# Expert 7 for the first 256 tokens, moved from the routing to the end of the program, and the last group's sums joined on VectorE

## The chip, the cores and the metric

One Trainium2 chip, one of its cores. The metric is the device time of one execution in microseconds (us); lower is better. All data are float32.

## The reference

Polysketch attention over 4 batches x 4 heads x 1088 tokens gives x, 4352 tokens x 128 features. A router then weighs all 8 experts for every token (Sinkhorn iterations), and every expert is computed for every token:

```python
logits = x @ w_gate                     # 4352 x 8
P = np.exp(logits - logits.max())
for _ in range(8):
    P /= P.sum(1, keepdims=True) + 1e-09
    P /= P.sum(0, keepdims=True) + 1e-09
    P *= N / E
for e in range(E):                      # w1[e]: 128 x 1024, w2[e]: 1024 x 128
    out += P[:, e:e + 1] * (np.maximum(x @ w1[e], 0.0) @ w2[e])
```

P is positive, so a token can be weighed before the first layer or after the second; the kernel does both, in different places.

## The kernel before

x is kept with features on partitions (`xT`, 128 x 4352). The expert work is cut in two.

**The unweighted items** (`groups`, `steps()`). They need no P, so they run on TensorE between the pieces of the attention and of the Sinkhorn routing; `fill(n)` and, after the routing, a loop take them step by step. Expert 0 is done here for all tokens. The first 256 tokens (`REST`) are done here for the experts 1 to 7 as well, one small item each of eight steps (order: 1, 2, 4, 3, 5, 6, 7). In a step `first` multiplies 128 of the 1024 hidden rows (line 787, ScalarE's Relu in line 789), and `second` multiplies the hidden rows of eight steps earlier (line 851). The last two items (`HELD = 2`, experts 6 and 7) keep their second products back: `held_product` (line 866) issues them among the weighted units. The sums land in `kept` (expert 0) and `kept_small` (experts 1 to 7); P weighs them much later (`rest_weigh`, on GpSimd), and `rest_out` turns them on VectorE and stores them, in the middle of the weighted part.

**The weighted units** (`weighted_events`). The other 4096 tokens go through the experts 1 to 7 in 8 groups of 512 tokens: 56 items, 112 units. Each unit uses a form of Strassen's seven products in both layers: `first_product` (line 1086), `taps` on ScalarE and VectorE (lines 1095 to 1107), `hsums` (lines 1113 to 1121), `second_products` (line 1136). All events have keys, and sorting the keys writes the program order of TensorE, VectorE and ScalarE; a period of 14 keys is one unit. Each engine runs its list strictly in that order, with semaphore waits where data or a PSUM bank is shared. GpSimd and SyncE also run in program order, but ahead of the others as far as their waits let them.

The combined weights that the seven products need ("forms") are made by `form_step`, four VectorE operations for each half of an expert (line 1048), and stored by `keep_formed`. Five halves (`AHEAD`) are made just before the weighted part, in the loop after the routing; six more (`IN_PLACE`) among the weighted units. `first_forms` (lines 988 to 992) makes the inputs of the first weighted item, from P as it comes back from DRAM (`pT`).

At the end of a group its sums lie in four PSUM banks (`ysums`) and have to be joined. For the groups but the last this is `group_end`, on ScalarE and VectorE while TensorE goes on. For the last group two copies and two additions bring them to SBUF (lines 1187, 1181), TensorE joins them with matrices of ones and zeros (`make_joins`, `join`, line 1237), VectorE turns the result (line 1213), and four transfers store it (line 757).

Names in the rows: `a` are the four banks of first products, `s` the four of second products, `w1f` and `w2f` the forms, `w2r` raw second weights, `hb` and `ht` hidden rows, `mid` a scratch tile.

Of the kernel before, what the change touches and what calls it, by code (L numbers as in the profile page):

```python
# [53 lines left out]
def kernel(  # L54
# [545 lines left out]
    def routing():  # L600
# [31 lines left out]
        for it in range(ITERS):  # L632
            rs = sk.tile([P, SA], F32, tag="rs", name="rs")
            nc.vector.reduce_sum(rs, pw, axis=AX.X)
            nc.vector.reciprocal(rs, rs)
            p1 = p1s[it % 2]
            nc.vector.scalar_tensor_tensor(p1[:, 0:SA], rs.unsqueeze(2).to_broadcast([P, SA, E]), UP,
                                           pw[:, :, 0:E], op0=Alu.mult, op1=Alu.mult)
            cs = sk.tile([P, E], F32, tag="cs", name="cs")
            nc.vector.reduce_sum(cs, p1.rearrange("p g e -> p e g"), axis=AX.X)  # L640
            yield 4.25
            pc = bank()[:, 0:E]
            for s in range(2):
# [236 lines left out]
    def steps():  # L880

        todo, sums_at, t = {}, {}, 0
        for k in range(len(blocks)):
            if k < len(blocks):
                j, q = blocks[k]
                g, e = items[j]
                n = groups[g][1]
                if q == 0:
                    prepare_w(j)
                if j == 0 and q == 2:  # L890
                    prepare_w(2)
                if j == 3 and q == 2:
                    small_load(2, wb[:, 3 * F:4 * F], wb[:, 4 * F:5 * F])
                if j == 7 and q == 0:
                    small_load(7, None, wb[:, 4 * F:5 * F])
# [41 lines left out]
    ENDING = {2: 42.6, 5: 43.6, 0: 46.6, 4: 47.6, 16: 50, 17: 51}  # L937
    X1, X2, Y1, Y2, T1, T3, T2, T4 = range(8)
    H0, H3, C12, H2_, D0, D1, D2 = range(7)
    D3 = C12  # L940
# [53 lines left out]
    def small_weights():  # L994

        spare = [pools[0].tile([P, 7, 2, NX], F32, tag="ht", name="ht").rearrange("p s a n -> p (s a n)") for _ in range(2)]
        xf0 = xfs[0].rearrange("p f n -> p (f n)")
        places = {3: (spare[0], 0, 1), 5: (spare[1], 0, 1), 4: (xf0, 0, 1)}
        for e, (t, i, k) in places.items():
            small_load(e, t[:, F * i:F * (i + 1)], t[:, F * k:F * (k + 1)])  # L1000
        small_load(6, spare[0][:, 2 * F:3 * F], wb[:, 5 * F:6 * F])
        small_load(7, spare[1][:, 2 * F:3 * F], None)

    def small_load(e, w1, w2):
        if w1 is not None:
# [158 lines left out]
    def rest_out(step):  # L1164
        yt = mid[:, 8 * NX:8 * NX + REST]
        if step:
            store(yt.rearrange("p (b d) -> p b d", d=32), 0, REST // 32, (nc.gpsimd,))
        else:
            nc.vector.transpose(out=yt, in_=kept[:, 0:REST])

    def group_end(g, step):

# [31 lines left out]
        elif step == 13:  # L1204
            add(y[upper, 0], z[upper, 2], z[upper, 1])
        elif step == 14:
            add(y[upper, 1], z[upper, 2], z[upper, 0])
        elif step == 15:
            y = y.rearrange("p s n -> p (s n)")
            add(y, y, kept[:, lo:lo + 2 * n])  # L1210
        elif step == 16:
            yt = turned_y[g] = mid[:, 4 * NX + 2 * NX * (g % 2):][:, 0:2 * n].rearrange("p (b d) -> p b d", d=32)
            nc.vector.transpose(out=yt.rearrange("p b d -> p (b d)"), in_=fbanks[0][:, 0:2 * n] if g == len(wgroups) - 1 else y.rearrange("p s n -> p (s n)"))
        elif step == 17:
            store(turned_y[g], lo // 32, (lo + 2 * n) // 32, (nc.gpsimd,) if g < len(wgroups) - 1 else (nc.sync, nc.scalar))

    turned_y, joins = {}, {}

    def make_joins():

        t = joins["t"] = mid[:, 4 * NX:6 * NX]
        tc.keep_in_program_order(nc.gpsimd.memset(t, 0.0))
        for half, lo, hi in ((lower, 0, 2), (lower, 3, 5), (upper, 3, 6), (upper, 7, 8)):
            tc.keep_in_program_order(nc.gpsimd.tensor_copy(
                t[half, H2 * lo:H2 * hi].rearrange("p (a d) -> p a d", d=H2),
                ident[half, half].unsqueeze(1).to_broadcast([H2, hi - lo, H2])))

    def join(g, step):

        lo, n, es = wgroups[g]  # L1230
        z = wb[:, 5 * F:5 * F + 4 * n].rearrange("p (s n) -> p s n", n=n)
        y = fbanks[0][:, 0:2 * n]

        def add(form, x, out, halves=(0, 1)):
            w = ident if form is None else joins["t"][:, H2 * form:H2 * form + P]
            for s in halves:
                nc.tensor.matmul(out[rows[s]], w[:, H2 * s:H2 * (s + 1)], x, start=x is kept_y, stop=True,  # L1237
                                 tile_position=(0, H2 * s), skip_group_check=True)

        kept_y = None  # L1240
        if step == 0:
            kept_y = kept[:, lo:lo + 2 * n]
            add(None, kept_y, y)
        elif step == 1:
            add(6, z[:, 2], y[:, 0:n], (1,))
            add(4, z[:, 2], y[:, n:])
            add(2, z[:, 3:4].to_broadcast([P, 2, n]), y.rearrange("p (a n) -> p a n", n=n), (1,))
        elif step == 2:
            add(0, z[:, 0], y[:, 0:n])
            add(3, z[:, 0], y[:, n:])  # L1250
            add(None, z[:, 1], y[:, 0:n])

    def weighted_events():
        out = []
# [23 lines left out]
        for k in range(len(units)):  # L1278
            b = PERIOD * k
            for r in range(2):  # L1280
                for m in AT:
                    if m in FIRST:
                        at(b + SHIFT * r + AT[m], first_product, k, r, m)
                    elif m in ("tm1", "tm5", "tu2", "rel", "c12", "c22"):
                        at(b + SHIFT * r + AT[m], taps, k, r, m)
                t, tasks = b + S_AT, list(range(7)) if k in firsts or k in lasts[:-1] else [6, 0, 4, 5, 1, 2, 3] if k == lasts[-1] else [0, 1, 6, 4, 5, 2, 3]
# [5 lines left out]
                at(b + (30.5 if m == "ts2" and k == len(units) - 2 else AT[m]), hsums, k, m)  # L1292
            if k in lasts:
                g = unit_of(k)[2]
                for n, key in (AFTER if k < lasts[-1] else ENDING).items():
                    at(b + key, group_end, g, n)
                if k == lasts[-1]:
                    at(b + 10, make_joins)
                    for n, key in enumerate((47.5, 48, 49)):
                        at(b + key, join, g, n)  # L1300
            if k in firsts:
                g = unit_of(k)[2]
                for step in range(wgroups[g][2][0]):
# [2 lines left out]
        for e in range(E):  # L1306
            at(420 + 28 * e, rest_weights, e)
            at(434 + 28 * e, rest_weigh, e)
        for step in range(2):
            at(660 + 14 * step, rest_out, step)  # L1310
        for n in range(2 * len(held)):
            at(HELD_AT + HELD_STEP * n, held_product, n)
        for n in range(HELD):
# [2 lines left out]
            at(end, held_sum, n)  # L1316
        return sorted(out, key=lambda x: x[:2])

    work = steps()
    owed, ran = [0.0], [0]  # L1320

# [30 lines left out]
    with tc.manual_schedule(engines={engines.DVE, engines.PE}):  # L1352
# [35 lines left out]
        forming = [lambda e=e, half=half, n=n: form_step(e - 1, half, n) for e, half in AHEAD for n in range(4)]  # L1388
        for n, (e, half) in enumerate(AHEAD):
            forming.insert(5 * n + 4, lambda e=e, half=half: keep_formed(e - 1, half))  # L1390
# [50 lines left out]
```

## Time and profile before

| | |
|---|---|
| Median of 3 runs | 904.93 us (902.96 to 906.27) |
| The profiled execution | 902.61 us, of which the span of the profile is 900.6 us |
| TensorE (PE) busy | 891.1 us, 99% of the span |
| VectorE (DVE), ScalarE (ACT), GpSimd (POOL) busy | 739.4, 526.2, 361.4 us |
| First weighted product | starts at 199.94 us |
| Last product, end of the joins, end of the span | 891.80, 895.84, 900.65 us |

A row of the timeline gives the start, the duration, the engine, the line of the kernel, the operation, the tile written and the tiles read, the shape, how many such instructions were merged into the row, and, in brackets, how long the engine had been idle before and whose end released it. One float32 product is two MATMUL entries. Their durations overlap, so a rate is read from the distance of starts.

### The profile page before, as it was taken

The page shows a single profiled execution, that of the slowest core. Times are in us where ns is not written, and L with a number is a line of the kernel's source. Part 1 is how long each engine was busy: PE and PEld are TensorE (multiplying, and loading weights), DVE is VectorE, ACT ScalarE, POOL GpSimd, SP SyncE. Part 2 cuts the span into 40 slices and gives each one's busy share as a digit, 9 for nine tenths or more (in the row PEclk, how much of TensorE's full clock was granted, in tenths as well). Part 3 has the DMA queues.
Part 4 walks back from the last instruction along what each step waited for, and adds up shares of the span by engine and source line. Part 5 has one row for each costly group of instructions (what it writes and reads, how often), then busy time and mean ns, then how long its engine had stood idle before and what let it go on. Part 6 is the DMA issues. An engine that isn't in the chain of part 4 may idle for free.

```text
span 900.6 us, 34646 instructions
## 1 busy us (share of the span) xinstructions
PE 891.1 (99%) x14664; PEld 718.5 (80%) x14664; DVE 739.4 (82%) x1160; ACT 526.2 (58%) x1276; POOL 361.4 (40%) x381
## 2 busy tenths in 40 slices
PE   8999999999999999999999999999999999999997
PEld 6786667688886998887878888778788887888885
DVE  7667678886889889799889988998888798889874
ACT  3353446465665765666666566666666666666562
POOL 3013310040444535366656454345443543544340
PEclk9999999999999999999999999999999999999999
DMA  9998492134677777677877767667776776777640
GB/s 260 295 284 271 151 330 75 42 148 135 172 211 246 240 222 218 210 217 209 241 232 218 222 206 217 201 214 222 218 221 188 219 218 206 234 212 218 188 127 13
DMA packets 150234, 183.97 MB, mean 204 GB/s; under 512 B 16352, under 2 KB 112368, under 8 KB 149696
## 3 DMA queue, kind: packets, MB, share of 16 engines
q1 hardware_dynamic: 143856, 164.17, 62.0%
q0 software_dynamic: 5024, 17.42, 5.6%
q8 instruction: 116, 1.90, 0.8%
q14 instruction: 38, 0.31, 0.1%
q10 hardware_dynamic: 1200, 0.16, 0.1%
HBM read 148.38 MB, written 18.65 MB: 185 GB/s over the span
## 4 chain that ended last, share of the span: by engine, by line
PE 96%; DVE 2%; DMA 1%; ACT 0%; SPq 0%; issue 0%; ACTq 0%; DVEq 0%
PE a L1086 37%; PE s L1136 37%; PE a L787 9%; PE s L851 8%; PE a L371 1%; PE s L866 1%; PE a L486 1%; DMA qx<-in_q_dram 1%; PE a L1237 0%; PE s L400 0%; PE a L450 0%; PE a L338 0%; DMA xd<-xt 0%; DMA xT<-xd 0%; PE s L416 0%
## 5 line engine op out<-in xcount | busy, mean ns | idle before, releaser
L1086 PE MATMUL a<-wb,w1f 64*64 64x256 f32 x4144 | 430.7, 377 | 0.1
L1086 PEld LDWEIGHTS a<-wb,w1f 64*64 64x64 f32 x4144 | 277.6, 133 | 34.0 <-issue 2.0
L1086 PE MATMUL a<-xf,w1f 64*64 64x256 f32 x2128 | 229.9, 377 | 0.1
L1100 ACT COPY a<-a 128x256 f32<-128x256 f32 x224 | 80.0, 357 | 214.2 <-PE a L1086 214.2
L1136 PE MATMUL s<-ht,w2r 64*64 64x256 f32 x1344 | 192.1, 377 | 0.0
L1136 PE MATMUL s<-hb,w2r 64*64 64x256 f32 x1344 | 190.7, 376 | 0.0
L201 POOL TENSOR_TENSOR wb<-wb 128x256 f32<-128x256 f32 (+1 forms) x115 | 127.9, 1113 | 121.6 <-DMA wb<-wb 106.8
L1136 PE MATMUL s<-ht,w2f 64*64 64x256 f32 x1216 | 159.6, 376 | 0.3 <-DVE w2f L1048 0.3
L1086 PEld LDWEIGHTS a<-xf,w1f 64*64 64x64 f32 x2128 | 142.5, 133 | 19.0 <-issue 1.1
L1136 PE MATMUL s<-hb,w2f 64*64 64x256 f32 x1216 | 157.5, 376 | 0.0
L1136 PEld LDWEIGHTS s<-ht,w2r 64*64 64x64 f32 x1344 | 113.9, 133 | 20.7 <-DVE ht L1121 0.4
L1136 PEld LDWEIGHTS s<-hb,w2r 64*64 64x64 f32 x1344 | 114.1, 133 | 18.6
L789 ACT ACTIVATE hb<-a 128x256 f32<-128x256 f32 (+3 forms) x152 | 66.2, 442 | 75.3 <-PE a L787 71.8
L1136 PEld LDWEIGHTS s<-ht,w2f 64*64 64x64 f32 x1216 | 100.1, 133 | 8.4 <-DVE w2f L1048 0.7
L1136 PEld LDWEIGHTS s<-hb,w2f 64*64 64x64 f32 x1216 | 99.7, 133 | 7.3
L787 PE MATMUL a<-xT,wb 128*64 128x416 f32 (+3 forms) x448 | 103.4, 459 | 0.0
L851 PE MATMUL s<-hb,wb 128*64 128x416 f32 (+3 forms) x408 | 99.8, 453 | 0.0
L201 POOL TENSOR_TENSOR xf<-xf 128x256 f32<-128x256 f32 (+1 forms) x62 | 69.0, 1116 | 70.4 <-DMA xf<-xf 50.2
L201 POOL TENSOR_TENSOR wb<-wb,xT 128x512 f32<-128x512 f32 x37 | 52.1, 1410 | 92.7 <-DMA wb<-pT 62.9
L1107 DVE TENSOR_TENSOR ht<-a,mid 128x256 f32<-128x256 f32 x112 | 47.2, 422 | 49.0 <-ACT a L1095 39.5
L1095 ACT COPY a<-a 128x256 f32<-128x256 f32 x224 | 80.0, 357 | 9.6 <-PE a L1086 1.0
L1098 ACT COPY mid<-a 128x256 f32<-128x256 f32 x224 | 84.7, 378 | 0.0
(203 smaller groups left out, 1648.5 us busy)
## 6 DMA issues: line engine op xcount, KB each, us to landing
w1f<-packed SPq DMA_DIRECT2D x204, 224.0 KB, 5.1
w2r<-in_moe_w_dram SPq DMA_DIRECT2D x56, 512.0 KB, 7.0
w2f<-packed SPq DMA_DIRECT2D x68, 256.0 KB, 5.0
wb<-pT SPq DMA_DIRECT2D x45, 256.0 KB, 4.5
wb<-wb SPq DMA_DIRECT2D x74, 128.0 KB, 4.0
hb<-packed SPq DMA_DIRECT2D x32, 256.0 KB, 6.4
xf<-pT SPq DMA_DIRECT2D x19, 256.0 KB, 4.5
xf<-xf SPq DMA_DIRECT2D x36, 128.0 KB, 4.3
```

Source lines behind the costliest of these rows:

```text
L201: tc.keep_in_program_order(nc.gpsimd.tensor_tensor(*args, op=op))
L371: nc.tensor.matmul(pv[64 * s:64 * (s + 1), i], kp[0:n, H * t + h].rearrange("p i j -> p (i j)"), vx[0:n, slots[h], t, :], start=(t == 0 an ...
L486: nc.tensor.matmul(pn[64 * s:64 * (s + 1), t, 2 * i:2 * i + 2].rearrange("p h d -> p (h d)"), ph[:, i, s, 64 * t:64 * (t + 1)], kvs[b % 2] ...
L787: nc.tensor.matmul(ph[sl], loaded_w[items[j][1]][0][:, P * f + H2 * s:P * f + H2 * (s + 1)], xT[:, lo:hi], start=True, stop=True, tile_pos ...
L789: nc.scalar.activation(out=out, in_=ph, func=Act.Relu)
L851: nc.tensor.matmul(sums[g][i][H2 * s:H2 * (s + 1)], w, x, start=c == 1, stop=c == per, tile_position=(0, H2 * s))
L1086: nc.tensor.matmul(half_of(r, b, c, n)[rows[s]], w1s[i][rows[r], 1 + form, u, H2 * s:H2 * (s + 1)], xf(i, x)[rows[r]], start=m == opens, s ...
L1095: nc.scalar.copy(b, a)
L1098: nc.scalar.copy(m5s[k, r], c)
L1100: nc.scalar.copy(d, a)
L1107: nc.vector.tensor_tensor(h[:, H3, r], d, m5s[k, r], op=Alu.add)
L1136: nc.tensor.matmul(place[rows[s]], w[form][rows[r], pair, u], h[rows[r], x, pair], start=task in (0, 4) and k in firsts, stop=True, tile_p ...
```

## The change

Expert 7 is taken out of the unweighted items, which leaves twelve of them, and the held items are now those of the experts 5 and 6. Its 256 tokens are now weighed before the first layer (`rest_weigh` writes them to a free part of `kept_small`). Its weights are loaded near the end into a part of `kept` that is free by then (`closing_load`). Four of its eight first products (`closing_first`) stand among the second products of the last unit but one, four behind the last second product of all. Its second products (`closing_second`) take the hidden rows as the stationary side, so that the result has tokens on partitions; a product with the identity brings the sums of the other seven experts, `kept`, into the same bank. This is done for two blocks of 128 tokens, and `closing_out` copies each block and stores it in four transfers. `rest_out` in the middle goes.

The last group's sums are joined by `last_end`: six ScalarE copies and thirteen VectorE additions, then the same turning and four transfers as before (now two by SyncE and two by GpSimd). `make_joins` and `join` go.

The forms of `AHEAD` start earlier: one entry of the list in each Sinkhorn iteration from the third on, the rest from seven steps earlier than before; `first_forms` comes six steps earlier. In the units 10 and 12 the order of the second products is changed, so that task 6 (which uses the form `S3_`) comes after the tasks 4 and 5.

```diff
             nc.vector.reduce_sum(cs, p1.rearrange("p g e -> p e g"), axis=AX.X)
+            if it > 1:
+                forming.pop(0)()
             yield 4.25
...
-              (2752, 416, [0]), (0, REST, [4]), (3584, 384, [0]), *((0, REST, [e]) for e in (3, 5, 6, 7))]
+              (2752, 416, [0]), (0, REST, [4]), (3584, 384, [0]), *((0, REST, [e]) for e in (3, 5, 6))]
...
     def rest_weigh(e):
+        if e == E - 1:
+            pool(kept_small[:, e - 1], xT[:, 0:REST], rest_room[0], op=Alu.mult)
+            return
...
+    CLOSING_AT = (24, 27, 30, 33, 48, 48.2, 48.4, 48.6)
+    closing_w = (kept[:, 2 * NX:2 * NX + F], kept[:, 2 * NX + F:2 * NX + 2 * F].rearrange("p (f d) -> p f d", d=DM))
...
+    def closing_h(c):
+        return hts[len(units) - 4][:, REST * c:REST * (c + 1)]
+
+    def closing_first(c):
+        ph = fbanks[c % 3][:, 0:REST]
+        for s in range(2):
+            nc.tensor.matmul(ph[rows[s]], closing_w[0][:, P * c + H2 * s:P * c + H2 * (s + 1)], kept_small[:, E - 2],
+                             start=True, stop=True, tile_position=(0, H2 * s), skip_group_check=True)
+        nc.scalar.activation(out=closing_h(c), in_=ph, func=Act.Relu)
+
+    def closing_second(b, c):
+        for s in range(2):
+            x = P * b + H2 * s
+            nc.tensor.matmul(fbanks[3][rows[s], P * b:P * (b + 1)],
+                             kept[:, x:x + H2] if c < 0 else closing_h(c)[:, x:x + H2],
+                             ident if c < 0 else closing_w[1][:, c], start=c < 0 and not b, stop=True,
+                             tile_position=(0, H2 * s), skip_group_check=True)
+
+    def closing_out(b):
+        y = mid[:, 8 * NX + P * b:8 * NX + P * (b + 1)]
+        nc.scalar.copy(y, fbanks[3][:, P * b:P * (b + 1)])
+        for a in range(4):
+            (nc.sync, nc.scalar)[a % 2].dma_start(out=..., in_=y[32 * a:32 * (a + 1)])
+
+    LAST_AT = (42.1, 42.6, 42.7, 42.8, 43, 43.1, 43.2, 43.3, 43.4, 44.1, 44.6, 44.7, 44.8, 44.9, 45, 45.1, 45.2, 47.1, 47.6, 48.1, 48.2)
+
+    def last_end(g, step):
...
+        (lambda: nc.scalar.copy(z[:, 2:4], s[1]),
+         lambda: add(z[:, 2:4], z[:, 2:4], s[3]),
+         lambda: nc.scalar.copy(x[upper, 0], z[lower, 3]),
+         lambda: nc.scalar.copy(x[lower, 0], z[upper, 2]),
+         lambda: add(y[upper, 1], z[upper, 3], z[upper, 2]),
+         lambda: add(y[lower, 1], z[lower, 2], k[lower, 1]),
+         lambda: add(y[:, 1], y[:, 1], x[:, 0]),
+         lambda: add(y[upper, 0], y[upper, 1], k[upper, 0]),
+         lambda: add(y[upper, 1], y[upper, 1], k[upper, 1]),
+         lambda: nc.scalar.copy(z[:, 0], s[0][:, 0]),
+         lambda: add(z[:, 0], z[:, 0], s[2][:, 0]),
+         lambda: nc.scalar.copy(x[upper, 1], z[lower, 0]),
+         lambda: nc.scalar.copy(x[lower, 1], z[upper, 0]),
+         lambda: add(y[:, 1], y[:, 1], z[:, 0]),
+         lambda: add(y[lower, 0], z[lower, 0], k[lower, 0]),
+         lambda: add(y[upper, 0], y[upper, 0], x[upper, 1]),
+         lambda: add(y[:, 1], y[:, 1], x[:, 1]),
+         lambda: add(y[:, 0], y[:, 0], s[0][:, 1]),
+         lambda: add(y[:, 0], y[:, 0], s[2][:, 1]),
+         lambda: group_end(g, 16),
+         lambda: group_end(g, 17))[step]()
...
-    def make_joins():
-    def join(g, step):
...
+ ... [0, 1, 4, 5, 6, 2, 3] if k in (10, 12) else [0, 1, 6, 4, 5, 2, 3]
...
+                for half in range(2):
+                    at(b - 8 + 8 * half, closing_load, half)
+                for n, key in enumerate(CLOSING_AT):
+                    at(b + key, closing_first, n)
+                for n in range(2):
+                    for c in range(-1, FO):
+                        at(b + 49 + n, closing_second, n, c)
+                    at(b + 49 + n, closing_out, n)
...
-        for step in range(2):
-            at(660 + 14 * step, rest_out, step)
...
-        among = {t0 + 10: [first_forms],
+        among = {t0 + 4: [first_forms],
...
-            if ran[0] > t0 + 3 and forming:
+            if ran[0] > t0 - 4 and forming:
```

More of the change, by code (lines that the diff above doesn't have):

```diff
@@ L894, in steps @@
                 if j == 7 and q == 0:
-                    small_load(7, None, wb[:, 4 * F:5 * F])
+                    small_load(5, None, wb[:, 4 * F:5 * F])
                 if q == 1 and j + 1 < len(items) and not direct_of(j + 1):
@@ L936 @@
              16: 170, 17: 184}
-    ENDING = {2: 42.6, 5: 43.6, 0: 46.6, 4: 47.6, 16: 50, 17: 51}
     X1, X2, Y1, Y2, T1, T3, T2, T4 = range(8)
@@ L997, in small_weights @@
         xf0 = xfs[0].rearrange("p f n -> p (f n)")
[L998 to L1002, printed above, removed]
+        small_load(3, spare[0][:, 0:F], spare[0][:, F:2 * F])
+        small_load(5, spare[1][:, 0:F], None)
+        small_load(4, xf0[:, 0:F], xf0[:, F:2 * F])
+        small_load(6, spare[1][:, F:2 * F], wb[:, 5 * F:6 * F])
     def small_load(e, w1, w2):
@@ L1162, in rest_weigh, with closing_load @@
             pool(kept[:, 0:REST], kept[:, 0:REST], y, op=Alu.add)
[L1164 to L1167, printed above, removed]
-        else:
-            nc.vector.transpose(out=yt, in_=kept[:, 0:REST])
+    CLOSING_AT = (24, 27, 30, 33, 48, 48.2, 48.4, 48.6)
+    closing_w = (kept[:, 2 * NX:2 * NX + F], kept[:, 2 * NX + F:2 * NX + 2 * F].rearrange("p (f d) -> p f d", d=DM))
+    def closing_load(half):
+        w1, w2 = closing_w
+        if half:
+            load_w2(E - 1, w2)
+        else:
+            tc.keep_in_program_order(nc.sync.dma_start(out=w1, in_=moe_w1[E - 1]))
@@ new lines, in closing_out @@
+    def closing_out(b):
+        y = mid[:, 8 * NX + P * b:8 * NX + P * (b + 1)]
+        nc.scalar.copy(y, fbanks[3][:, P * b:P * (b + 1)])
+        for a in range(4):
+            (nc.sync, nc.scalar)[a % 2].dma_start(out=AP(tensor=out.tensor, offset=out[4 * b + a, 0].offset, ap=[[SA * DM, 32], [1, DM]]),
+                                                  in_=y[32 * a:32 * (a + 1)])
+    LAST_AT = (42.1, 42.6, 42.7, 42.8, 43, 43.1, 43.2, 43.3, 43.4, 44.1, 44.6, 44.7, 44.8, 44.9, 45, 45.1, 45.2, 47.1, 47.6, 48.1, 48.2)
@@ new lines, in last_end, with add @@
+    def last_end(g, step):
+        lo, n, es = wgroups[g]
+        if ("w", g) not in parts:
+            parts["w", g] = room("w", 2 * n)
+        z = wb[:, 5 * F:5 * F + 4 * n].rearrange("p (s n) -> p s n", n=n)
+        y = wb[:, 4 * F + F // 2:5 * F][:, 0:2 * n].rearrange("p (s n) -> p s n", n=n)
+        x = parts["w", g].rearrange("p (s n) -> p s n", n=n)
+        k = kept[:, lo:lo + 2 * n].rearrange("p (s n) -> p s n", n=n)
+        s = [ysums[g][b].rearrange("p (s n) -> p s n", n=n) for b in range(4)]
+        def add(out, a, b):
+            nc.vector.tensor_tensor(out, a, b, op=Alu.add)
+        (lambda: nc.scalar.copy(z[:, 2:4], s[1]),
[19 more added lines that the diff above has]
+         lambda: group_end(g, 17))[step]()
@@ L1212, in group_end @@
             yt = turned_y[g] = mid[:, 4 * NX + 2 * NX * (g % 2):][:, 0:2 * n].rearrange("p (b d) -> p b d", d=32)
-            nc.vector.transpose(out=yt.rearrange("p b d -> p (b d)"), in_=fbanks[0][:, 0:2 * n] if g == len(wgroups) - 1 else y.rearrange("p s n -> p (s n)"))
+            nc.vector.transpose(out=yt.rearrange("p b d -> p (b d)"), in_=y.rearrange("p s n -> p (s n)"))
         elif step == 17:
-            store(turned_y[g], lo // 32, (lo + 2 * n) // 32, (nc.gpsimd,) if g < len(wgroups) - 1 else (nc.sync, nc.scalar))
-    turned_y, joins = {}, {}
-    def make_joins():
[L1221 to L1226, printed above, removed]
-    def join(g, step):
[L1230 to L1251, printed above, removed]
+            store(turned_y[g], lo // 32, (lo + 2 * n) // 32, (nc.gpsimd,) if g < len(wgroups) - 1 else (nc.sync, nc.gpsimd))
+    turned_y = {}
     def weighted_events():
@@ L1285, in weighted_events @@
                         at(b + SHIFT * r + AT[m], taps, k, r, m)
-                t, tasks = b + S_AT, list(range(7)) if k in firsts or k in lasts[:-1] else [6, 0, 4, 5, 1, 2, 3] if k == lasts[-1] else [0, 1, 6, 4, 5, 2, 3]
+                t, tasks = b + S_AT, list(range(7)) if k in firsts or k in lasts[:-1] else [6, 0, 4, 5, 1, 2, 3] if k == lasts[-1] else [0, 1, 4, 5, 6, 2, 3] if k in (10, 12) else [0, 1, 6, 4, 5, 2, 3]
                 while tasks:
@@ L1294, in weighted_events @@
                 g = unit_of(k)[2]
[L1295 to L1300, printed above, removed]
+                if k < lasts[-1]:
+                    for n, key in AFTER.items():
+                        at(b + key, group_end, g, n)
+                    continue
+                for n, key in enumerate(LAST_AT):
+                    at(b + key, last_end, g, n)
+                for half in range(2):
[6 more added lines that the diff above has]
+                    at(b + 49 + n, closing_out, n)
             if k in firsts:
@@ L1317, in weighted_events @@
         return sorted(out, key=lambda x: x[:2])
+    forming = []
+    for e, i in AHEAD:
+        forming.extend(lambda e=e, i=i, n=n: form_step(e - 1, i, n) for n in range(4))
+        forming.append(lambda e=e, i=i: keep_formed(e - 1, i))
     work = steps()
@@ L1387 @@
         turn_first()
-        forming = [lambda e=e, half=half, n=n: form_step(e - 1, half, n) for e, half in AHEAD for n in range(4)]
-        for n, (e, half) in enumerate(AHEAD):
-            forming.insert(5 * n + 4, lambda e=e, half=half: keep_formed(e - 1, half))
-        among = {t0 + 10: [first_forms],
+        among = {t0 + 4: [first_forms],
                  t0 + 12: [lambda do=do: do(1) for do in (weights, weighted, turn, xsums)]}
```

## The prediction

> **What bounds the kernel now.** I read the page first: busy times, and the chain that ended last.
>
> ```profile
> PE 891.1 (99%) x14664; PEld 718.5 (80%) x14664; DVE 739.4 (82%) x1160; ACT 526.2 (58%) x1276; POOL 361.4 (40%) x381
> PE 96%; DVE 2%; DMA 1%; ACT 0%; SPq 0%; issue 0%; ACTq 0%; DVEq 0%
> ```
>
> TensorE (PE) carries the chain from end to end. So work that leaves PE is worth its full time, wherever it stood, as long as no other engine becomes late by it. Second, PE's waits; in the whole weighted part there are two:
>
> ```profile
> PE s L1136 <- DVE hb L1048: 1.1, 1, 1.1
> PE s L1136 <- DVE w2f L1048: 0.3, 1, 0.3
> ```
>
> Both are second products that wait for a form made by VectorE (DVE). Third, PE's timeline where the weighted part begins:
>
> ```profile
> 194.12 0.65 PE L787 MATMUL a<-xT,ht 128*64 128x256 f32 x4
> 194.55 0.65 PE L851 MATMUL s<-hb,ht 128*64 128x256 f32 x4
> 194.99 0.65 PE L787 MATMUL a<-xT,ht 128*64 128x256 f32 x4
> 195.42 0.65 PE L851 MATMUL s<-hb,ht 128*64 128x256 f32 x4
> 195.85 3.67 PE L787 MATMUL a<-xT,ht 128*64 128x256 f32 x32
> 199.45 0.66 PE L1407 MATMUL a<-zeros 64*64 64x256 f32 x8
> 199.94 0.38 PE L1086 MATMUL a<-xf,w1f 64*64 64x256 f32 x2
> ```
>
> By the distance of starts a step's first product (four entries) takes 0.43 us and its second product 0.43; nothing waits. Fourth, the other engines at the end (timeline):
>
> ```profile
> 890.19 0.59 ACT L1187 COPY wb<-s 128x512 f32<-128x512 f32 x1 [3.78 <-PE s L1136]
> 890.80 0.69 DVE L1181 TENSOR_TENSOR wb<-wb,s 128x512 f32<-128x512 f32 x1 [1.69 <-ACT wb L1187]
> 895.87 0.72 DVE L1213 STREAM_TRANSPOSE mid<-a 128x512 f32<-128x512 f32 x1 [3.08 <-PE a L1237]
> 896.61 0.88 SPq L757 DMA_DIRECT2D out_dram<-mid  x2
> 896.61 0.96 ACTq L757 DMA_DIRECT2D out_dram<-mid  x2
> ```
>
> The last products end at 891.80 and the joins at 895.84 (chain), turning ends at 896.59, the span at 900.65. By the table of stages the data of the last store move from 897.4 to 899.0, so 0.8 us pass before them and 1.6 behind them.
>
> **The change, part by part.** The profiled execution took 902.61, 2.0 over its span and 0.26% under the median of 904.93; I work in its times and carry the difference over to the median.
>
> *Front.* Item 7 leaves: eight steps of 0.43 + 0.43, so 6.9 us, and the first weighted product moves from 199.94 to about 193.0. Held products stay the same in number. What covers this: DVE must be through its own list when the first tap comes, 4.45 us after the first weighted product (the add of line 1107 started at 204.39), so at 197.5 now. From the last turning in the routing, which ended at 171.97, its list is six subtractions of line 802 (2.10 + 2.15), `first_forms` (4.3 with GpSimd beside it), six sums of group 8 (6 x 0.56, and 2.9 more, since one took 3.50 beside GpSimd) and 15 forms (0.34 to 0.42 each, 5.7): 20.6 us, so 192.5, or 198.7 if all 6.2 us of waits of before (0.86 + 3.34 + 1.96) came back. Since five forms more can fill these waits, I take no cost; the bounds are 0 and 1.2. Unit 0 itself needs only `first_forms`, whose P had landed by about 179; they should end near 183. GpSimd now stores two halves of forms ahead of the last sums for item 1, which should be ready by about 194 (two sums of 1.3 and 1.1 us each side of a 4 us transfer) and are needed at 205.
>
> *Forms in the routing.* Five DVE operations of 0.42 us, each behind the column sums of an iteration and ahead of three subtractions. PE's small product needs those sums, which are finished first: no wait. The reciprocal behind them can come 0.4 later; PE's next column product stood about 2 us behind its sums, so the five are hidden; unhidden they cost 2.1. They move the last turning, and P's way through DRAM, by 0.4; `first_forms` had about 10 us to spare.
>
> *Tasks 4 and 5 ahead of 6 in units 10 and 12.* The form that came too late is `S3_`, the last to be made there. Task 6 now comes four keys later, 1.7 us, against waits of 1.1 and 0.3: minus 1.4 (0 if another wait takes their place).
>
> *Middle.* One turning, four stores on GpSimd's queue and one GpSimd product go. None was on the chain: 0. Held copies, weights of expert 7 (two loads of 512 KB, queued behind the last w2f issued at 863.5, 7.0 us to landing, needed after 885): 0, with 14 us of cover.
>
> *End.* Times here are those of before, from which the 8.3 us above are taken off last. Unit 110's second products start at 884.74 and take 3.0. Among them now stand four closing first products, 4 x 0.43 = 1.7, and I add 0.4 for the changes between whole-height and half-height products (no row prices that; 0 to 0.8). Unit 111's thus start at 889.85 instead of 887.7, and the copy of the first pair of sums, 2.45 later, at 892.3. Call this T; before it was 890.19, and the last product ended at T + 1.6.
>
> Now comes what I hold to be the price of the change. In the order of the changed program, task 2 of row half 0 waits for the ScalarE (ACT) copy of the other half of the same bank, and task 2 of row half 1 for the DVE addition that reads its bank. Both stand deep in `last_end`. ACT: copy 0.59; DVE addition to T + 1.30; two copies (0.36, 0.27 apart) to T + 1.98; then the copy in question to T + 2.25. DVE: additions at T + 1.33, 1.67, 2.12 (waits for ACT's copy), 2.57, 3.02 (each needs the one before), and the one in question T + 3.36 to 3.78. So PE stops at about T + 0.7, does tasks 2 and 3 of one half from 2.3 to 3.15, stops again to 3.8, and ends the last product at T + 4.7 instead of 1.6: 3.1 us of waits.
>
> Behind it: four closing first products 1.7 (T + 6.4; ACT keeps up, the last Relu ends at 7.0); block 0, identity and eight products of 128 columns: 0.215 each, half the 0.43 of 256 columns, 1.95 (T + 8.35); ACT copy of 128 x 128, 0.25 by the slope between 0.36 for 256 and 0.59 for 512, with 0.2 ahead of it for the drain (T + 8.8); block 1 waits for that copy, since it uses the same bank, then 1.95 (T + 10.8); copy to T + 11.25; two issues on each queue, first 0.8 to the data, then 0.4 for a second issue and little data (256 pieces against 2112), then 1.6 to the end: T + 14.1 = 906.4. Against 900.65 that is plus 5.75. In it, the joins' 4.04 us on PE and the turning are gone. `last_end` itself ends at about T + 6.8 on DVE, its store near T + 10.5: hidden under the closing products, with 3 us of cover.
>
> Sum: -6.9 - 1.4 + 5.75 = -2.55, so 900.1 in profiled terms and 902.4 as median. The gain of the front is for the most part paid back at the end: PE's work of item 7 is not less there (3.44 + 3.87), only the joins are saved, and more than half of that goes into waits.
>
> **Rivals.** *The waits at the end do not bind* (the copy and the addition come earlier than I chain them, or part of the waits overlaps). Then the 3.1 us and block 1's 0.45 go: -6.1, 898.8. For it: PE has practically no wait in the profile of before, and nothing shows a stop at the end. Against: the waits are written in the program, and the durations come from rows.
>
> *The clock falls* (slower than before). After the joins PE has nothing to do, and the table of stages shows the granted clock (after PEclk's place, before the DMA share):
>
> ```profile
> 898.20:898.60 0.40, 0.00 (x0) 0.00 (x0) 0.00 (x0) 0.00 (x0) 0.00 (x0) 1.00 1.20 192
> 898.60:899.00 0.40, 0.00 (x0) 0.00 (x0) 0.00 (x0) 0.00 (x0) 0.00 (x0) 0.66 1.09 167
> 899.00:899.20 0.20, 0.00 (x0) 0.00 (x0) 0.00 (x0) 0.00 (x0) 0.00 (x0) 0.50 0.06 8
> ```
>
> It halves near 898.7, 2.9 us after PE stopped. If the stops of 1.6 and 0.65 us with little work between them are long enough for that, the 6.4 us of matmuls behind (0.85 + 1.7 + 3.9) take twice as long: +6.4, 908.8. It decides from a stop of about 2.9 us; I expect 1.6. The Trainium skill (TensorE: Matmul & The Clock Gate, Part 1) says that a free-running window of about 3.4 us without work halves the clock; the trace agrees with the half, and with the time as far as a free-running window allows, and by that rule two stops this short would not do it.
>
> *DVE is late at the start of the weighted part* (forms, or GpSimd beside DVE): PE waits at the first taps and the front gives 3 to 5 us instead of 6.9: 904.3 to 906.3. For it: additions in that stretch took 3.50 and 1.38 us where 0.55 and 0.42 are usual. Against: the count above leaves 5 us.
>
> *The reordering brings nothing* (the form is late all the same): +1.4, 903.8, inside the forecast.
>
> **How the numbers follow.** My forecast 0.64, waits that do not bind 0.18, late DVE 0.10, clock 0.06, else 0.02. About 0.5%, 4.5 us, is what a measurement of this kernel can tell from no change. Only the second case passes it on the fast side, and an end of the forecast's own spread (0 to 0.8, 0 to 1.2, chains read 1 us wrong); the clock case hardly reaches it on the slow side. Faster 0.20, same 0.73, slower 0.07. The range goes from the second case's lower side to the late DVE's upper side, 898.3 to 906.8.
>
> **What would show it.** First weighted product near 193; no wait of line 1136 for line 1048; in the last 15 us, PE waits of about 1.5 and 0.7 us at line 1136 for ACT and DVE, a wait of about 0.5 for the copy of line 1197, and 2.8 us from that line's last copy to the end. A first weighted product later than 194, a last stretch without those waits, or a clock below 1.00 ahead of the last store would each prove the step wrong that names it.

## The result, and the profile after

The changed kernel is slower by 0.5%: 910.67 us median of 7 runs (907.80 to 911.18) against 904.93 (902.96 to 908.21), a ratio of 1.0053, 95% interval 1.0032 to 1.0074. The forecast was 902.4, range 898.3 to 906.8, so it is missed on the slow side, by 8.3 us. The profiled execution took 907.80, its span 905.81: 5.2 over the one of before.

From the page, the busy line and the chain that ended last:

```profile
PE 896.1 (99%) x14680; PEld 720.3 (80%) x14680; DVE 744.0 (82%) x1170; ACT 527.7 (58%) x1281; POOL 362.3 (40%) x373
PE 95%; DVE 3%; issue 1%; ACT 1%; DMA 1%; SPq 0%; POOL 0%; ACTq 0%; DVEq 0%; POOLq 0%
```

TensorE still carries the chain, and it is busy 5.0 us longer than before, with 16 MATMUL entries (8 products) more. Busy time that grows by more than the work does points to the clock. PE's waits from 195 us to the end (line, releaser, sum, times, longest):

```profile
PE s L1136 <- ACT wb L1227: 2.1, 1, 2.1
PE s L1136 <- DVE wb L1216: 0.5, 1, 0.5
PE a L1190 <- ACT mid L1197: 0.4, 1, 0.4
PE a L1086 <- DVE ht L1107: 0.3, 1, 0.3
```

The two waits for line 1048 are gone, and three waits stand at the end, those that the prediction named. PE's timeline, the first weighted product and the end:

```profile
193.93 0.38 PE L1086 MATMUL a<-xf,w1f 64*64 64x256 f32 x2
890.18 1.56 PE L1136 MATMUL s<-hb,w2r 64*64 64x256 f32 x8 [2.07 <-ACT wb L1227]
892.22 1.97 PE L1136 MATMUL s<-hb,w2r 64*64 64x256 f32 x8 [0.47 <-DVE wb L1216]
894.12 3.58 PE L1183 MATMUL a<-kept,kept 128*64 128x256 f32 x16
900.03 0.44 PE L1190 MATMUL a<-ident,kept 128*64 128x128 f32 x4 [0.37 <-ACT mid L1197]
```

Read the durations: eight matmuls of 64 rows take 1.56 and 1.97 us, and four closing first products (16 entries) 3.58, where 0.43 each would make 1.7. ScalarE's rows for the copy of the first pair of sums (the prediction's T) and the last copy:

```profile
887.71 0.59 ACT L1218 COPY wb<-s 128x512 f32<-128x512 f32 x1 [1.49 <-PE s L1136]
902.26 0.27 ACT L1197 COPY mid<-a 128x128 f32<-128x128 f32 x1 [2.29 <-PE a L1190]
```

The table of stages (stretch, its length, then the busy time of PE, PEld, DVE, ACT and POOL, then the granted clock) says why. Its stretches are cut at the edges of the clock's record:

```profile
887.22:890.64 3.42, 1.35 (x24) 0.67 (x16) 1.80 (x4) 1.66 (x4) 0.00 (x0) 1.00 0.00 0
890.64:894.05 3.41, 2.94 (x14) 0.98 (x10) 3.21 (x9) 0.81 (x2) 0.00 (x0) 0.50 0.01 2
894.05:897.46 3.41, 3.41 (x18) 1.95 (x18) 1.27 (x3) 1.15 (x3) 1.29 (x2) 0.50 0.27 54
897.46:900.88 3.42, 3.05 (x54) 2.74 (x52) 0.00 (x0) 0.65 (x2) 0.00 (x0) 1.00 0.15 29
```

The clock is halved from 890.64 to 897.46, over almost all of the work that stands between the stop and the closing second products.

**Where the time went.** Spans of one kernel wander by some us, so I cut each profiled execution at three marks of PE: the first small product of the routing's iterations (line 644 before, 646 after), the first weighted product, and the start of the last weighted first product. Every run below is in the table.

| kernel | start to routing | to first weighted | weighted | end | span |
|---|---|---|---|---|---|
| before | 122.67 | 77.27 | 685.45 | 15.27 | 900.65 |
| after | 122.84 | 71.09 | 685.22 | 26.65 | 905.81 |
| e1_late | 124.23 | 71.06 | 684.91 | 21.30 | 901.51 |
| e2_busy | 123.82 | 71.06 | 685.87 | 24.15 | 904.90 |
| e3_no_routing_forms | 123.45 | 70.36 | 684.85 | 26.95 | 905.60 |
| e4_behind | 122.14 | 71.05 | 686.82 | 25.02 | 905.04 |
| e5_before_order | 122.90 | 77.28 | 686.21 | 15.27 | 901.66 |
| e6_both | 122.51 | 71.07 | 687.65 | 19.35 | 900.59 |
| e7_both_old_order | 123.52 | 71.07 | 686.40 | 19.37 | 900.36 |
| e8_busy_two | 124.46 | 71.07 | 687.47 | 25.82 | 908.82 |
| e9_both_no_forms | 122.27 | 70.36 | 687.11 | 19.42 | 899.17 |
| e10_copy_first | 123.29 | 70.37 | 684.78 | 17.96 | 896.39 |

The first and third columns scatter by 2 to 3 us among kernels that are equal there. The second repeats to 0.04 us among the kernels with one front, and the fourth to 0.3 where nothing at the end was changed. So the second and fourth are what can be explained: after against before, they are -6.18 and +11.38. (The expectations below give some ends from spans read to 0.1 us, which differ from the table by up to 0.06.)

### The profile page after: what moved, and what is told of

It is laid out like the page before. It is cut to its first block, busy times and chain, and to the rows that moved or that the text cites. A ratio compares the mean times of both kernels' runs of the same rounds, so it can differ in the third digit from the quotient of the medians.

```text
span 905.8 us, 34686 instructions
## 1 busy us (share of the span) xinstructions
PE 896.1 (99%) x14680; PEld 720.3 (80%) x14680; DVE 744.0 (82%) x1170; ACT 527.7 (58%) x1281; POOL 362.3 (40%) x373
## 4 chain that ended last, share of the span: by engine, by line
PE 95%; DVE 3%; issue 1%; ACT 1%; DMA 1%; SPq 0%; POOL 0%; ACTq 0%; DVEq 0%; POOLq 0%
PE a L1086 37%; PE s L1136 36%; PE a L789 8%; PE s L853 7%; PE a L371 1%; PE s L868 1%; PE a L486 1%; PE a L119 1%; PE a L1183 1%; PE a L1190 0%; PE a L338 0%; DVE hb L1115 0%; PE s L400 0%; PE a L450 0%; DVE hb L1121 0%
## 5 line engine op out<-in xcount | busy, mean ns | idle before, releaser
L1086 PEld LDWEIGHTS a<-wb,w1f 64*64 64x64 f32 x4144 | 271.4, 133 | 36.2 <-issue 3.2
L201 POOL TENSOR_TENSOR wb<-wb 128x256 f32<-128x256 f32 (+1 forms) x115 | 131.0, 1141 | 118.7 <-DMA wb<-wb 91.8
L1136 PEld LDWEIGHTS s<-ht,w2r 64*64 64x64 f32 x1344 | 113.6, 133 | 18.9
L791 ACT ACTIVATE hb<-a 128x256 f32<-128x256 f32 (+3 forms) x144 | 63.2, 445 | 72.9 <-PE a L789 69.9
L201 POOL TENSOR_TENSOR xf<-xf 128x256 f32<-128x256 f32 (+1 forms) x62 | 72.2, 1167 | 68.3 <-DMA xf<-xf 43.8
```

What stands on the lines that cost most here:

```text
L201: tc.keep_in_program_order(nc.gpsimd.tensor_tensor(*args, op=op))
L791: nc.scalar.activation(out=out, in_=ph, func=Act.Relu)
L1086: nc.tensor.matmul(half_of(r, b, c, n)[rows[s]], w1s[i][rows[r], 1 + form, u, H2 * s:H2 * (s + 1)], xf(i, x)[rows[r]], start=m == opens, s ...
L1136: nc.tensor.matmul(place[rows[s]], w[form][rows[r], pair, u], h[rows[r], x, pair], start=task in (0, 4) and k in firsts, stop=True, tile_p ...
```

## Experiments

A task, below, is one of the seven second products of a unit; TensorE does each for two row halves, and a half-height product uses only one of them. T is, as in the prediction, the start of the copy of the first pair of sums.

The theory after the result: the two bank waits stop TensorE, and this stop, though shorter than the 2.9 us that the prediction took as the point of decision, halves the clock. Rivals: the clock falls for another cause, or the end is longer only for the work that was moved there.

**e1_late: the waits taken away.** The copies and additions of `last_end` that the last tasks waited for come behind them in program order.

```diff
-LAST_AT = (..., 43.4, 44.1, 44.6, 44.7, 44.8, 44.9, 45, 45.1, 45.2, 47.1, 47.6, 48.1, 48.2)
+LAST_AT = (..., 43.4, 48.7, 48.71, 48.72, 48.73, 48.74, 48.75, 48.76, 48.77, 48.78, 48.79, 49.5, 49.5)
```

> Ten of the steps of last_end, from the copy after the first pair of copies on to the store, stand behind the four closing first products in the listed order, so that tasks 2 and 3 of unit 111 no longer wait for ScalarE or VectorE. Theory 1 (the two bank waits of 2.07 and 0.47 us stop TensorE, and the stop halves its clock for 6.83 us, 3.4 us of work): both waits go, the clock stays 1.00 up to the last product, and the profiled span falls by 2.5 + 3.4 = 5.9 us to about 900; less by up to 1 if last_end's store is then the last thing to land. Rival A (the halved clock has nothing to do with the wait and comes whatever is done at the end): only 2.5 go, 903.3. Rival B (the end is longer only for the work moved there): less than 1 us goes, 905.

Measured: 904.66 us, ratio to before 1.0006 (0.9995 to 1.0017). Both waits are gone, the clock stays at 1.00 to the last product, and the end shrinks by 5.35 us (the span by 4.3, since the first column happens to be 1.4 later). PE's timeline:

```profile
890.00 1.95 PE L1183 MATMUL a<-kept,kept 128*64 128x256 f32 x16
```

The same four closing products that took 3.58 us take 1.95, with starts 0.44 apart. Rival A (only the 2.5 us of the waits) and rival B (less than 1 us) fall. The gain stops at 5.35 and not 5.9: the store of `last_end` is now late, and the last closing store on SyncE's queue behind it issues at 897.42, 0.63 us after its data are there (taken up at e10_copy_first).

**e2_busy: the wait left, the stop filled.**

```diff
+    def keep_busy(n):
+        for _ in range(n):
+            for s in range(2):
+                nc.tensor.matmul(fbanks[3][rows[s], 0:REST], ident[:, H2 * s:H2 * (s + 1)], kept[:, 0:REST],
+                                 start=True, stop=True, tile_position=(0, H2 * s), skip_group_check=True)
...
+                at(b + 44.95, keep_busy, 5)
```

> Ten half-height matmuls of 256 columns whose results nobody uses stand just ahead of task 2 of unit 111, where TensorE waits 2.07 us for ScalarE's copy; the wait itself stays as it is. They take about 5 x 0.21 to 5 x 0.43 us, so 1.1 to 2.1 of the 2.07 us. Theory 1 (the stop halves the clock): clock 1.00 up to the last product, span down by 3.0 to 3.4 us to about 902.6, although TensorE does more work. Rival A (the clock falls for another cause, such as the load of the end): clock 0.50 for some 6.8 us as before, span the same or up to 0.4 longer. Rival C (a stop of 1 us is enough): clock still 0.50, later by the length of the added products.

Measured: 906.66 us, 1.0032 (1.0019 to 1.0045); the granted clock of all 7 runs is 1.0. ScalarE's copy at T and PE's timeline:

```profile
889.30 0.59 ACT L1224 COPY wb<-s 128x512 f32<-128x512 f32 x1 [1.49 <-PE s L1136]
889.64 2.38 PE L1198 MATMUL a<-kept,ident 128*64 128x256 f32 x20
891.95 1.08 PE L1136 MATMUL s<-hb,w2r 64*64 64x256 f32 x8
893.83 1.08 PE L1136 MATMUL s<-hb,w2r 64*64 64x256 f32 x8 [0.80 <-DVE wb L1222]
```

TensorE does 2.3 us more work, and the end is 2.50 us shorter. The ratios of the two kernels overlap in their intervals; the clock and the length of the end are what shows it. This is the plainest proof that the stop sets the clock: what the last tasks wait for comes as before, and work put into the stop keeps the clock up. It also sizes the loss: the last task starts T + 4.53 here and T + 4.51 in the changed kernel, because VectorE's chain sets that moment at either clock (the slow task of 1.56 us is hidden, the wait in front of the last one shrinks). What the clock costs is what comes behind: 892.22 to 897.46 at half, 5.24 / 2 = 2.6 us.

**e4_behind: no closing products among unit 110's.**

```diff
-CLOSING_AT = (24, 27, 30, 33, 48, 48.2, 48.4, 48.6)
+CLOSING_AT = (48, 48.1, 48.2, 48.3, 48.4, 48.5, 48.6, 48.65)
```

> The four closing first products that stood among unit 110's second products stand behind the last second product, with the other four. Theory (a whole-height product of 128 rows among half-height ones costs about 0.9 us instead of the 0.43 of a step's own): the copy of the first pair of sums comes 3.8 us earlier against the last first product (4.8 behind it instead of 8.56), the eight closing first products in one go take 8 x 0.43 = 3.4 at full clock, and the span falls by about 2, apart from what the clock does. Rival (they cost 0.43 anywhere, and the 3.76 us lie in something else): the same to 0.3. The stop for last_end stays, so the clock is expected at 0.50 here too, over as many us as in the changed kernel.

Measured: 907.01 us, 1.0033 (1.0022 to 1.0044). The end is 1.63 us shorter, against 2. ScalarE's and PE's timeline:

```profile
884.82 0.58 ACT L1218 COPY wb<-s 128x512 f32<-128x512 f32 x1 [3.78 <-PE s L1136]
887.29 1.08 PE L1136 MATMUL s<-hb,w2r 64*64 64x256 f32 x8 [1.72 <-ACT wb L1227]
891.23 5.70 PE L1183 MATMUL a<-kept,kept 128*64 128x256 f32 x32
```

T now comes 4.80 us behind the start of the last first product, exactly as in the kernel before, instead of 8.56. So the four closing products had cost 3.76 us, 0.94 each: in the changed kernel they start 1.60 apart, with the next task 0.59 behind each, where 0.43 is usual. In a row they take 0.44 (e6_both below: 32 entries from 887.59 to the next group at 891.09). The clock falls here as well, for 6.83 us, after a wait of 1.72 us.

**e3_no_routing_forms.**

```diff
-            if it > 1:
-                forming.pop(0)()
```

> The five forms that VectorE makes inside the routing's iterations are taken out of them and made with the rest behind the routing. Theory (they stand ahead of subtractions for which TensorE waits, and cost the 0.85 us by which the front gave less than 6.9): the first weighted product moves from 193.93 to about 193.1, and the span falls by 0.85 unless VectorE, with five more forms of 0.42 us to make in front of the weighted part, is late at its first taps. Rival (the 0.85 us is GpSimd or DMA in the routing, not these forms): the first weighted product stays at 193.9. Second rival (VectorE late): 193.1, and TensorE waits of up to 2.1 us in the first units.

Measured: 907.32 us, 1.0045 (1.0027 to 1.0063); the end is that of the changed kernel. The first weighted product stands at 193.81, which by itself tells nothing: equal fronts gave 193.19 to 195.53. Counted from the routing's first small product it is 70.36 against 71.05 to 71.09 in the seven kernels with the forms. The timeline of one iteration in the changed kernel:

```profile
147.18 0.41 DVE L1048 TENSOR_TENSOR w1f<-w1f 128x256 f32<-128x256 f32 x1
147.51 1.21 DVE L804 TENSOR_TENSOR hb<-hb 128x416 f32<-128x416 f32 x2
148.15 0.13 PEld L853 LDWEIGHTS s<-hb,wb 128*64 128x64 f32 x1 [0.74 <-DVE hb L804]
```

and the same subtractions without the forms:

```profile
147.43 1.21 DVE L802 TENSOR_TENSOR hb<-hb 128x416 f32<-128x416 f32 x2
```

The form stands ahead of the subtractions, and a held second product of PE waits for these. The subtraction starts 0.91 us behind the start of the column sums (146.60) with the form, and 0.57 without (146.86). Over the routing the five forms cost 0.71 us. The second rival, a late VectorE at the first units, did not come: PE's first wait behind 193.81 is one of 0.26 us at 236.18.

**e5_before_order: the reordering alone, on the kernel before.** Units 10 and 12 do tasks 4 and 5 ahead of 6.

```diff
-... else [0, 1, 6, 4, 5, 2, 3]
+... else [0, 1, 4, 5, 6, 2, 3] if k in (10, 12) else [0, 1, 6, 4, 5, 2, 3]
```

> The kernel before, with one edit alone: tasks 4 and 5 ahead of task 6 in units 10 and 12. Theory (the reordering is worth what the prediction gave it): the two waits for line 1048 go, the stretch from the first to the last weighted first product is 684.0 instead of 685.45 us, the time 0.15% less. Rival (another wait takes their place or the stretch varies by as much from run to run): 685.2 to 685.5. The front is that of the kernel before, so this run also says how much the first weighted product of an unchanged front moves from run to run: 199.94 was the one value so far, and four runs with the changed front gave 193.93, 195.30, 194.88 and 193.19. If the changed front gives 6.9 less, it should come near 201.2; if the 0.85 us are lost in the routing, near 200.2.

Measured: 904.16 us, 0.9998 (0.9987 to 1.0009): no difference in the whole time, which by this interval could hide about 1 us. The weighted stretch was 686.21, not 684.0. PE's waits in it:

```profile
PE s L1136 <- issue: 1.0, 1, 1.0
PE a L1086 <- DVE ht L1107: 0.7, 1, 0.7
```

The waits for the form are gone, and a wait for VectorE's additions at the taps (at 281.20) has taken part of their place. The other wait, 1.0, stands at 237.98, ahead of the units in question, and the profile names nobody that ended it; it makes the weighted stretch longer and has nothing to do with the order. So a shorter stretch is worth a look: from the first product of unit 8 to that of unit 16, between which both waits of the kernel before lie (at 278.95 and 291.54), it takes 50.71 us before and 49.75 here, 0.96 less. As to the front, 77.28 against 77.27: the loss in the routing belongs to the change.

**e6_both and e7_both_old_order: the end mended, with the new and the old order.** e6_both joins the edits of e1_late and e4_behind and puts the second closing block in another bank; e7 is the same with the order of before in units 10 and 12.

```diff
-            nc.tensor.matmul(fbanks[3][rows[s], P * b:P * (b + 1)],
+            nc.tensor.matmul(fbanks[3 - b][rows[s], 0:P],
...
-                             ident if c < 0 else closing_w[1][:, c], start=c < 0 and not b, stop=True,
+                             ident if c < 0 else closing_w[1][:, c], start=c < 0, stop=True,
...
-        nc.scalar.copy(y, fbanks[3][:, P * b:P * (b + 1)])
+        nc.scalar.copy(y, fbanks[3 - b][:, 0:P])
```

> The changed kernel with three edits at its end: the ten late steps of last_end behind the closing first products, all eight closing first products behind the last second product, and the second block of closing sums in another bank, so that it does not wait for the copy of the first. Theory: the clock stays 1.00 to the last product, and from the last weighted first product to the end it takes 21.29 - (3.76 - 1.72) - 0.37 = 18.9 us (26.65 in the changed kernel, 15.21 in the kernel before). With a front of 5.6 less and a middle of 0.2 to 0.4 less that is about 2.2 us under the kernel before, ratio 0.9975. Rival (the chain of VectorE's joins, T + 7.7 and its store, becomes what ends last): 19.5 to 20.5 and the same time as before. Rival (something else than waits, clock and those four products lengthens the end): 21 or more.

> As the run before it in this list, but with tasks in units 10 and 12 in the order of the kernel before. Theory (the reordering saves waits that the earlier front makes longer): the stretch from first to last weighted first product grows by 1.0 to 2.0 us, with waits of lines 1136 for 1048 of 1.4 us or more, and the time by about 0.15%. Rival (it is worth nothing): the same to 0.3 us.

Measured: e6_both 901.81 us, 0.9967 (0.9954 to 0.998), so it is faster than both kernels; e7_both_old_order 902.55, 0.9979 (0.9968 to 0.9991). The end took 19.35 and 19.37 us instead of 18.9: the rival of VectorE's chain is true in part (next experiment). The two intervals overlap, and the whole weighted stretch was even shorter with the old order. PE's two waits of line 1136 in that stretch of e7:

```profile
PE s L1136 <- DVE hb L1048: 0.7, 1, 0.7
PE s L1136 <- DVE w2f L1048: 0.7, 1, 0.7
```

So the old order does bring the waits back, 1.4 us in sum. From unit 8 to unit 16 the old order takes 50.95 us here and the new one 50.13 in e6_both, 0.82 less; in all ten profiled kernels with the new order this stretch is 49.23 to 50.13, in the two with the old one 50.71 and 50.95. At unit 28 the two pairs still differ by 0.88 (e5 and before) and 0.72 us; further on, stretches of equal kernels scatter by 2 us. So the reordering probably brings 0.8 to 1.0 us where it stands, from one profiled execution of each kernel; what of it reaches the end is below what these measurements resolve. Why it isn't 1.4 can be seen in part: VectorE is busy 44.0 of the 50.7 us before and 45.4 of 49.8 in e5, and new waits of 0.7 us for it stand at the taps in e5 and e6_both.

**e9_both_no_forms and e10_copy_first.** e9 is e6_both without the routing's forms. e10 adds to this the copy of the first half of the second pair of sums (and its addition) ahead of the closing Relus on ScalarE, behind the last product.

```diff
-CLOSING_AT = (48, 48.1, 48.2, 48.3, 48.4, 48.5, 48.6, 48.65)
+CLOSING_AT = (48.1, 48.2, 48.21, 48.22, 48.23, 48.5, 48.6, 48.65)
...
-LAST_AT = (..., 43.4, 48.7, 48.71, 48.72, 48.73, 48.74, 48.75, 48.76, 48.77, 48.78, 48.79, 49.5, 49.5)
+LAST_AT = (..., 43.4, 48.05, 48.06, 48.25, 48.26, 48.27, 48.28, 48.29, 48.3, 48.31, 48.32, 49, 49)
```

> The kernel with the three edits at the end (late steps of last_end, eight closing first products behind the last product, second bank), and also without the five forms in the routing's iterations. Measured from the first small product of the routing's iterations to the first weighted product, all seven profiled kernels with these forms took 71.05 to 71.09 us, the one without them 70.36, and the two with the front of before 77.27 and 77.28. Theory: 70.36 again, the end 19.4 us, the time 0.7 us under that of the three edits alone, about 901.1, ratio 0.996. Rival (VectorE is late at the first taps by as much): the same time as the three edits alone, 901.8.

> As the run before it in this list, but ScalarE's copy of the first half of the second pair of sums stands ahead of the closing Relus instead of behind all eight, still behind the last second product (so that TensorE doesn't wait for it), and the two copies that need the addition behind it stand among the Relus. Without this, VectorE waited 1.92 us for that copy, its last transposition ended at 895.64, and the store issued behind it held back the last closing store on SyncE's queue by 1.1 us. Theory: VectorE's chain ends 1.9 us earlier, the last copy of ScalarE is followed by the end after 3.3 us instead of 5.1, the end takes 17.6 us instead of 19.4, the time about 899.4, ratio 0.994. Rival (the Relus that now come later stop TensorE): up to 0.8 of the 1.8 us are lost, with waits of line 1181 for ScalarE.

Measured: e9_both_no_forms 901.19 us, 0.9966 (0.9952 to 0.998); its front is 70.36 again, its end 19.42. 0.7 us is under what the ratio resolves; the front's repeated value shows it. e10_copy_first 900.97 us, 0.9958 (0.9945 to 0.9971), end 17.96 against 17.6 expected: the best version, though its interval overlaps those of e6 and e9. What e10 mended, in e6_both's timeline of ScalarE and SyncE:

```profile
891.59 0.37 ACT L1227 COPY wb<-s 128x256 f32<-128x256 f32 x1
895.67 0.86 SPq L759 DMA_DIRECT2D out_dram<-mid  x2
896.62 0.93 SPq L1199 DMA_DIRECT2D out_dram<-mid  x2
```

The copy had to wait behind eight Relus, VectorE behind the copy, and the last closing store on SyncE's queue behind the store of `last_end`, 1.1 us after its data were ready (ScalarE's own issue was at 895.54). In e10:

```profile
891.94 1.89 SPq L1197 DMA_DIRECT2D out_dram<-mid  x4
```

`last_end`'s store now issues at 890.95, ahead of both closing blocks, and four closing issues stand behind it on the same queue; I take this for the 0.4 us still missing, but no run tests it.

**e8_busy_two: a shorter stop.** `keep_busy` with 2 instead of 5, on the changed kernel.

> As with the ten idle matmuls ahead of task 2, but with four of them (0.95 us by the rate seen there), so that TensorE still stops for about 1.1 us. The clock's edges so far lie on a grid of 3.413 us; it halved at the end of windows in which TensorE was busy 0.52, 1.35 and 1.52 us, and did not after 2.29, 2.61 and 3.03. Theory (the share of a grid window decides): busy at least 2.2 in each, clock 1.00, the end 24.2 us long as with ten. Rival (any stop over 1 us is enough): clock 0.50 for 6.83 us, the end 26.5 us long.

Measured: 910.51 us, 1.0055 (1.0033 to 1.0076). My theory was wrong as put: the clock fell, for 3.41 us, and the end took 25.82. The rival's 6.83 us and 26.5 did not come either. In 4 of the 5 runs the mean clock was 0.996 to 0.998, in one 1.0 (907.03 us). The wait for ScalarE was 1.05 us, the one for VectorE 0.95. The table of stages of e8:

```profile
893.72:897.14 3.42, 2.16 (x18) 1.02 (x20) 2.80 (x8) 1.06 (x3) 0.00 (x0) 1.00 0.01 2
897.14:900.55 3.41, 3.41 (x19) 1.91 (x20) 2.00 (x5) 1.15 (x3) 0.94 (x2) 0.50 0.11 21
```

and of e9_both_no_forms, around PE's last product:

```profile
892.14:895.55 3.41, 1.56 (x30) 1.31 (x25) 1.91 (x5) 0.27 (x1) 1.11 (x2) 1.00 0.22 48
```

The windows here and below are cut where the clock can change, 3.413 us apart (the next section says how that is known). A window with 2.16 us of busy time ended in the half clock, and one with 1.56 did not (e9's clock fell only at 898.97). The difference I see: in e8 nearly all of it is tasks of one row half, so half the array, while e9's are whole-height. If half-height work alone counts half, the windows behind which the clock fell hold 1.12 (after), 0.98 (e4_behind), 1.1 (e8) and 1.34 (after, 900.88 to 904.29, whole-height), and those where it stayed 1.56 (e9), 1.58 (e10) and 2.0 (e2_busy). The rows for the last window of the changed kernel, for e4_behind and for e2_busy:

```profile
900.88:904.29 3.41, 1.34 (x26) 1.09 (x21) 0.00 (x0) 0.27 (x1) 0.00 (x0) 1.00 0.14 37
885.13:888.55 3.42, 1.52 (x16) 0.47 (x8) 2.52 (x6) 1.34 (x4) 0.00 (x0) 1.00 0.01 2
890.57:893.98 3.41, 2.61 (x24) 1.33 (x22) 2.74 (x8) 1.24 (x4) 0.00 (x0) 1.00 0.01 2
```

That sorts these windows, but it was read off afterwards and no run was made to test it.

## Why the prediction was wrong

The forecast in profiled terms was 900.1, measured 907.80: 7.7 us, of which 0.2 lie ahead of the change, 0.7 in the front, 1.2 in the weighted stretch and 5.6 at the end.

*Front, -6.9 forecast, -6.18 measured.* The -6.9 itself is right: without the routing's forms the front is 77.27 - 70.36 = 6.91 shorter. The failed step is "so the five are hidden". I looked for cover at PE's small product and its next column product, and missed who else stands behind VectorE there: the held second products, which wait for the three subtractions that I had myself named as standing behind the form. 0.71 of the 2.1 us that I gave as the unhidden price came through.

*Tasks 4 and 5 ahead of 6, -1.4 forecast; -0.23 in the weighted stretch (685.22 against 685.45), which wanders by more.* Both waits went, as said. Over the units 8 to 16, which hold them, the new order took 0.82 and 0.96 us less in the two pairs that differ in it alone: I took the sum of the waits as their worth, although VectorE was busy there for most of the time and part of the delay reappeared at the taps. The rival "the reordering brings nothing" is not shown; that the whole time did not move is within what 1 us can hide. Middle, 0: right as far as the wander allows.

*End, +5.75 forecast, +11.38 measured.* Four terms, with what they measured:

- T, behind the start of the last first product: 6.91 forecast (892.3 - 885.39), 8.56 measured, +1.65. The 0.4 us for the changes between whole-height and half-height products, with bounds 0 to 0.8, was 2.0 (3.76 - 1.72). No row priced it, and the bounds should have been wider.
- The waits, last task at T + 3.8 forecast, T + 4.51 measured, +0.7. The mechanism and the order of the waits were right: 2.07 and 0.47 instead of 1.6 and 0.65. Most of the 0.7 stands at VectorE's addition that waits for ScalarE's copies: it started at 890.37, T + 2.66, where the chain had T + 2.12.
- The clock, 0 forecast, 2.6 measured. The rival "the clock falls" was the true case, with a chance of 0.06, and its price (6.4) was too high for the place: part of the slow work lay under VectorE's chain, and the clock returned before the closing second products.
- Behind the last task, 10.3 forecast, 13.59 - 2.6 = 11.0 measured, +0.7: the last copy to the end took 3.28 instead of 2.85; the rest is spread over several steps and stays open.

The largest step that failed is the clock's: it was put at nothing in the sum. Behind its small chance stood "It decides from a stop of about 2.9 us"; stops of 2.07 and 0.47 us, with little work between them, cost 2.6 us by the clock. The figure of 2.9 came from one halving after PE had ended for good: 895.84 to 898.73 is the distance from the stop to the next edge of the clock, not a limit. All edges in these runs lie on a grid of 3.413 us, and the window that ended at 898.73 had begun at 895.32. What I should have asked is how empty a window can get, and the answer in the trace of before was only that 0.52 of 3.41 us is too little. The Trainium skill (TensorE: Matmul & The Clock Gate, Part 1) speaks of a free-running window of about 3.4 us and of at least one idle window ahead of the half clock. The trace agrees with window and half, but not with the idle window: stops of 2.07 and 1.72 us were enough, so the measurement decides. It also says that the monitor goes by how busy TensorE was. By plain busy time that does not sort the windows above (2.16 us fell, 1.56 did not); it does so only if half-height work is counted half, which is not tested.

The late VectorE at the start of the weighted part did not come, and the rival that the waits do not bind did not hold either: they bound, with 2.07 and 0.47 us.

## What to carry to other kernels

Ahead of moving work to the end of a kernel, write out for each of its instructions who waits for the bank it reads: here an addition and a copy that read one half of a bank held up products that write the other half, by 0.47 and 2.07 us. These stops cost more than their length, because the clock halved over the few us of work behind them: fill such a stop with idle products, or better, place what it waits for behind the products (here the two edits made the end shorter by 2.5 and 5.4 us). The length of a wait is not yet its worth when the engine that it waits for is busy nearly all the time (here 1.4 us of waits gave at most about 1.0), a stretch must be cut so that it holds all the waits in question, and a stretch cut at two marks near the change tells 0.7 us where whole times scatter by 5.

## What was not expected of the hardware

The clock was halved for 6.83 us (two windows of 3.413) after a stop of 2.07 us, in the profiled execution of the changed kernel; the mean clock of its seven runs, 0.995 to 0.997, lies below that of every run of the kernel before (0.998 to 1.000). A whole-height product of 0.43 us put among half-height ones cost 0.94. Ten matmuls with unused results made the end shorter, 24.15 us against 26.65.
